# Attention scores by one 64-row matmul a head, even heads on the upper half of the TensorE array and odd heads on the lower

## The chip, the cores and the metric

The program runs on one core of one Trainium2 chip. The metric is the device time of one execution in microseconds (us), the median over several runs. The engines are named as the profile names them: PE is TensorE's matmul, PEld its load of the stationary operand, DVE is VectorE, ACT is ScalarE, POOL is GpSimd, SP is SyncE, which issues most DMAs.

## The reference

Eight batches of eight heads, 576 positions, 64 values a head. Keys and values are averaged over 8 neighbouring positions, so that 72 pooled positions are left; every query attends to them; the result goes through two feed-forward layers with 4608 tokens.

```python
k_p = k.reshape(B, H, Sp, 8, D).mean(axis=3)          # Sp = 72, D = 64
v_p = v.reshape(B, H, Sp, 8, D).mean(axis=3)
scores = scale * np.matmul(q, k_p.transpose(0, 1, 3, 2))
attn = softmax(scores)                                 # + 1e-9 in the sum
x = np.matmul(attn, v_p)  ->  (4608, 512)
h = relu(x @ w_in);  x = (h * h) @ w_out               # 512 -> 2048 -> 512
h = x @ w_in2;  g = where(h >= 1, h, where(h <= -1, 0, (h + 1)**2 / 4))
out = g @ w_out2
```

All is float32. The large products are made of three float32r products of a high and a low part each; the scores are plain float32 products.

## The kernel before

The 4608 tokens go through the attention and the first layer in nine chunks of 512 (`c`), each chunk in tiles of at most 128 tokens. A tile (`tokens`) goes through these steps: `t0` transposes its queries on PE (`qps`) and ACT copies them into `T.qT`, which holds for each pair `p` of heads the 128 rows "64 of the even head, 64 of the odd head"; then the scores, then the softmax (`soft`: DVE takes the maximum, then subtracts it, and `t3` has ACT take the exponent; for seven tiles `T.scalar` is set and ACT does one head at a time), then `t4` (DVE sums, inverts, multiplies into `A`), then `t56` (PE transposes `A` into `aps` and `lps`). `pv_two` and `pv_pair` multiply with the values (`pvps`), which gives the first layer's input x.

The scores use a block-diagonal matrix `kBD`: for each pair `p` of heads it is 128 rows by 144 columns, with the pooled keys of the even head in rows 0 to 63 and columns 0 to 71, those of the odd head in rows 64 to 127 and columns 72 to 143, and zeros, set once at the start by a DVE memset, in the two other blocks. One matmul with all 128 rows of contraction gives the scores of both heads of a pair. `k_T` (first batch) and `k_T_all` (the other seven) transpose the pooled keys on PE (`kps`), and ACT copies each half to its place:

```python
nc.scalar.activation(out=kBD[0:64, :, 0:SP_], in_=pv[0:64], func=AF.Copy, scale=ESCALE)
nc.scalar.activation(out=kBD[64:P, :, SP_:], in_=pv[64:P], func=AF.Copy, scale=ESCALE)
```

A tile's scores come in one of two forms. `t1` (the tiles of chunk 0 and the first three of chunk 1) takes one PSUM bank for two pairs of heads, does their two matmuls and then their softmax, and is called twice a tile. `t12` (the last two tiles of chunk 1 and all later ones) takes two banks, does all four matmuls at once and then the softmax of each bank. A tile that reaches over the end of a batch does its scores in two pieces, the first of which uses only the first 64 columns of `T.qT` as stationary operand. In all there are 40 pieces: 33 through `t12`, of which 29 have 128 tokens in the stationary operand and 4 have 64, and 7 through `t1`. `T.qT` is the stationary operand of each score matmul, the keys are the moving one.

The first layer runs beside this: for each of 16 slices `f` of its width there are 12 matmuls of 512 columns into `hp` (`h_mm`, lines 703 to 705) and, two slices later, 12 into four banks `y` (`y1_mm`, line 729). The order of the work on each engine is not written by hand: each piece of work is a generator that yields the engine it wants and a cost, and the class `Order` plays them through and issues them in the order that these costs give. The costs are numbers in the source (`yield "PE", 0.5` ahead of the scores of `t12`, `yield "ACT", 0.41` ahead of a copy of keys); changing one can move other instructions. After chunk 8 the second layer follows (`product`, line 963, and `y2_unit`, lines 972 to 974), which has no attention beside it.

Of the kernel before, what the change touches and what calls it, by code (L numbers as in the profile page):

```python
# [8 lines left out]
F32 = mybir.dt.float32  # L9
# [4 lines left out]
AF = mybir.ActivationFunctionType  # L14
ALU = mybir.AluOpType
AX = mybir.AxisListType
# [3 lines left out]
P = 128  # L20
# [131 lines left out]
def pooled_attention_moe_moe2(  # L152
# [13 lines left out]
    nc = tc.nc  # L166
    B, H, S, D = q.shape
# [3 lines left out]
    SP_ = S // POOL  # L171
    NP = H // 2
# [15 lines left out]
    ESCALE = 1.0 / (POOL * D ** 0.5)  # L188
# [15 lines left out]
    att = att_pool.__enter__()  # L204
# [5 lines left out]
    for d in range(3):  # L210
        m = mask[RL * d:RL * d + RL]
        nc.gpsimd.affine_select(
            out=m, in_=m, compare_op=ALU.is_ge, fill=0.0, base=0, channel_multiplier=1, pattern=[[-KL, HL]]
        )
        nc.gpsimd.affine_select(
            out=m, in_=m, compare_op=ALU.is_ge, fill=0.0, base=KL - 1, channel_multiplier=-1, pattern=[[KL, HL]]
# [10 lines left out]
    for c in range(NC):  # L227
        gs, col = [], 0
        while col < N:
            n = min(NG, N - col) if c > 1 else min(NG, N - col, S - (c * N + col) % S)  # L230
            ts = []
            for at in range(0, n, P):
                pieces, o, most = [], 0, min(P, n - at)
                while o < most:
                    b, start = divmod(c * N + col + at + o, S)
# [15 lines left out]
    def w_tile(f, dtype, name):  # L251
        return wpool.tile([P, 4 * DM], dtype, tag=f"w{f}", name=name)
# [77 lines left out]
        )  # L330


    kBD = att.tile([P, NP, 2 * SP_], F32, name="kBD")
    VH = att.tile([P, NP, 2, D], F32R, name="VH")
    VL = att.tile([P, NP, 2, D], F32R, name="VL")
    for t in (VH, VL):
        nc.vector.memset(t.bitcast(F32), 0.0)
    nc.vector.memset(kBD, 0.0)
    LV = att.tile([P, 2, HL, D], F32R, name="LV")[:3 * RL]
    att.tile([P, 8], F32, name="gap")  # L340

# [57 lines left out]
    def k_T(b, p):  # L399
        tag, ps = yield from take_ps("kps")  # L400
        kp = kp_t.pop((b, p))
        yield "PE", 0.35 * order.pe
        nc.tensor.transpose(ps[:, :SP_], kp[:SP_].rearrange("s h d -> s (h d)"), ident[:SP_, :SP_])
        yield "ACT", 0.45
        nc.scalar.activation(out=kBD[0:64, p, 0:SP_], in_=ps[0:64, :SP_], func=AF.Copy, scale=ESCALE)
        nc.scalar.activation(out=kBD[64:P, p, SP_:], in_=ps[64:P, :SP_], func=AF.Copy, scale=ESCALE)
        order.give("ps", tag)
        order.signal("k", b, p)

    def k_T_all(b):  # L410
        tag, ps = yield from take_ps("kps")
        yield "PE", 0.3
        for p in range(NP):
            kp = kp_t.pop((b, p))
            nc.tensor.transpose(
                ps[:, p * SP_:(p + 1) * SP_], kp[:SP_].rearrange("s h d -> s (h d)"), ident[:SP_, :SP_]
            )
        pv = ps[:, :NP * SP_].rearrange("q (p s) -> q p s", p=NP)
        yield "ACT", 0.41
        nc.scalar.activation(out=kBD[0:64, :, 0:SP_], in_=pv[0:64], func=AF.Copy, scale=ESCALE)  # L420
        yield "ACT", 0.41
        nc.scalar.activation(out=kBD[64:P, :, SP_:], in_=pv[64:P], func=AF.Copy, scale=ESCALE)
        order.give("ps", tag)
        for p in range(NP):
            order.signal("k", b, p)
# [44 lines left out]
    def take_ps(name):  # L470
        tag = yield "take", ("ps",)
        return tag, (psy if tag[0] == "y" else psa).tile([P, 512], F32, tag=tag, name=name)

    def tile_of(T, what):
# [12 lines left out]
        ps=("a0", "a1", "y0", "y1", "y2", "y3"), att=("",), at=("",), kv=("",), two=("",), yo=("", ""), job=("",) * 4  # L487
# [31 lines left out]
    def scores_of(T):  # L519
        if T.E is None:  # L520
            T.E = tile_of(T, "E")
            T.mx = att.tile([P, H, 1], F32, tag="mx", name="mx", bufs=4)
            if T.scalar:
                T.sm = att.tile([P, H, 1], F32, tag="sm", name="sm", bufs=4)

    def soft(T, ps, g, r):
        E, mx = T.E, T.mx
        hs = slice(4 * g, 4 * g + 4)
        sv = ps[r, :4 * SP_].rearrange("p (h s) -> p h s", h=4)

        yield "DVE", 0.47
        nc.vector.tensor_reduce(out=mx[r, hs], in_=sv, axis=AX.X, op=ALU.max, negate=True)
        if T.scalar:
            for h in range(4 * g, 4 * g + 4):
                yield "ACT", 0.3
                nc.scalar.activation(
                    out=E[r, h], in_=sv[:, h % 4], func=AF.Exp, bias=mx[r, h], accum_out=T.sm[r, h]
                )
        else:
            yield "DVE", 0.47  # L540
            nc.vector.tensor_tensor(
                out=E[r, hs], in0=sv, in1=mx[r, hs].to_broadcast([r.stop - r.start, 4, SP_]), op=ALU.add
            )

    def t1(T, g, r):
        scores_of(T)
        tag, ps = yield from take_ps("sps")
        yield "PE", order.pe
        for j in range(2):
            p = 2 * g + j  # L550
            nc.tensor.matmul(
                out=ps[:r.stop, j * 2 * SP_:(j + 1) * 2 * SP_], lhsT=T.qT[:, p, :r.stop], rhs=kBD[:, p, :],
                start=True, stop=True,
            )
        yield from soft(T, ps, g, r)
        order.give("ps", tag)

    def t12(T, r):
        scores_of(T)
        taken = []  # L560
        for g in range(2):
            taken.append((yield from take_ps("sps")))
        yield "PE", 0.5
        for g, (_, ps) in enumerate(taken):
            for j in range(2):
                p = 2 * g + j
                nc.tensor.matmul(  # L567
                    out=ps[:r.stop, j * 2 * SP_:(j + 1) * 2 * SP_], lhsT=T.qT[:, p, :r.stop], rhs=kBD[:, p, :],
                    start=True, stop=True,
                )  # L570
        for g, (tag, ps) in enumerate(taken):
            yield from soft(T, ps, g, r)
            order.give("ps", tag)

    def t3(T):
# [402 lines left out]
    with tc.manual_schedule():  # L978

        lent = []  # L980
        for i in range(4):
            t = w_tile(KF - 4 + i, F32, "lent").rearrange("p (e a n) -> p e a n", e=2, a=2)
            lent += [t[:, 0], t[:, 1]]
        qw = w_tile(11, F32, "qraw").rearrange("p (r n) -> p r n", r=QR)
        T, T1 = tiles[0], tiles[1]
# [4 lines left out]
        t = w_tile(8, F32R, "lent")  # L990
# [87 lines left out]
        def keys0(b, p, eng):  # L1078
            yield ev("k raw", b, p)
            yield from k_pool(b, p, eng)  # L1080
            yield from k_T(b, p)
# [25 lines left out]
        def keys_T(b, last):  # L1107
            yield ev("scores", last, b - 1)
            for p in range(NP):
                yield ev("kp", b, p)  # L1110
            yield from k_T_all(b)
# [20 lines left out]
        def tokens(t):  # L1132
# [27 lines left out]
            for b, _, o, m in t.pieces:  # L1160
                for p in range(NP):
                    yield ev("k", b, p)
                r = slice(o, o + m)
                if t in pace or t in T1[3:]:
                    yield from t12(t, r)
                else:
                    for g in range(2):
                        yield from t1(t, g, r)
                order.signal("scores", t, b)
# [294 lines left out]
        for i in range(C2 * PAIRS):  # L1464
            c, j = divmod(i, PAIRS)
            for k in range(M7):
# [14 lines left out]
                if loads2 and k in (2, 5):  # L1481
                    _, load, n = loads2.pop(0)
# [44 lines left out]
```

## Time and profile before

| | us |
|---|---|
| median of 3 runs | 1716.55 (1716.06 to 1721.89) |
| the profiled execution, its own time | 1715.73 |
| its span, first to last instruction | 1714.0 |
| PE busy | 1685.9 |
| ACT busy | 862.0 |
| DVE busy | 929.1 |

The profiled execution's time is its span and 1.7 us around it, and 0.8 us under the median of the runs. Line numbers in rows of the trace are those of the kernel before. In a row of a matmul, `128*64 128x144` means 128 rows of contraction, 64 columns of the stationary operand, and a moving operand of 128 partitions by 144 columns. A float32 matmul stands as two records in the trace: 160 score matmuls are written and 320 are recorded.

### The profile page before, as it was taken

How to read it: one execution, taken by the hardware profiler on the slowest of the kernel's cores; microseconds unless marked ns; L12 is line 12 of the kernel's file. 1: busy time of each engine (PE TensorE's matmuls, PEld its weight loads, DVE VectorE, ACT ScalarE, POOL GpSimd, SP SyncE). 2: the span in 40 equal slices, each digit the busy share in tenths (PEclk: the TensorE clock that was granted, in tenths of full speed). 3: DMA queues.
4: the chain of work that ended last, by engine and by line, in shares of the span. 5: the costliest groups of instructions: out<-in, count | busy, mean ns of one | idle time of the engine just before them, and what ended most of it. 6: DMA issues, size and time to landing. Idle time of an engine off the chain costs nothing.

```text
span 1714.0 us, 22862 instructions
## 1 busy us (share of the span) xinstructions
PE 1685.9 (98%) x8366; PEld 1463.2 (85%) x8366; DVE 929.1 (54%) x1811; ACT 862.0 (50%) x1704; POOL 170.3 (10%) x185
## 2 busy tenths in 40 slices
PE   5999999999999999999999999999999999999999
PEld 4888888888888888888888899899999899999897
DVE  7896757666666565655422344544444444444544
ACT  5885545545455555455333444544444444444544
POOL 3322221023111132210000000000000000000000
PEclk6899999999999999999999999999999999999999
DMA  9844767677766666666468464614424325225312
GB/s 247 238 172 129 231 204 230 207 233 225 232 223 194 216 211 205 210 181 206 129 232 299 180 232 147 229 54 151 163 74 156 133 74 181 108 74 203 111 50 86
DMA packets 207616, 302.44 MB, mean 176 GB/s; under 512 B 65552, under 2 KB 155920, under 8 KB 192912
## 3 DMA queue, kind: packets, MB, share of 16 engines
q1 hardware_dynamic: 202896, 292.59, 52.6%
q10 hardware_dynamic: 4608, 8.39, 1.3%
q8 instruction: 66, 1.08, 0.2%
q14 instruction: 46, 0.38, 0.1%
HBM read 219.68 MB, written 81.26 MB: 176 GB/s over the span
## 4 chain that ended last, share of the span: by engine, by line
PE 95%; DMA 3%; SPq 1%; DVE 1%; POOL 1%; ACT 0%; issue 0%; POOLq 0%
PE y L729 22%; PE h L963 21%; PE y L973 8%; PE y L972 8%; PE y L974 8%; PE hp L703 7%; PE hp L705 7%; PE hp L704 7%; PE pvps L666 2%; PE sps L567 2%; PE qps L511 1%; PE aps L616 1%; DMA qraw<-in_q_dram 1%; DMA kv<-in_v_dram 1%; DMA lent<-in_v_dram 0%; DMA w<-in_moe_w_in_dram 0%
## 5 line engine op out<-in xcount | busy, mean ns | idle before, releaser
L729 PE MATMUL y<-gh,w 128*128 128x512 f32 (+1 forms) x1168 | 302.5, 392 | 0.0
L963 PE MATMUL h<-xc,s 128*128 128x384 f32 x1440 | 290.0, 336 | 0.0
L963 PEld LDWEIGHTS h<-xc,s 128*128 128x128 f32 x1440 | 257.2, 188 | 19.2 <-DVE yo L1410 0.4
L729 PEld LDWEIGHTS y<-gh,w 128*128 128x128 f32 x1168 | 212.5, 188 | 40.4 <-issue 0.4
L703 PE MATMUL hp<-x,w 128*128 128x512 f32 (+1 forms) x584 | 232.3, 398 | 0.0
L704 PE MATMUL hp<-x,w 128*128 128x512 f32 (+1 forms) x584 | 226.6, 388 | 0.3 <-DVE w L301 0.3
L705 PE MATMUL hp<-x,w 128*128 128x512 f32 (+1 forms) x584 | 226.9, 388 | 0.0
L973 PE MATMUL y<-x,g 128*128 128x512 f32 x576 | 226.1, 392 | 0.0
L972 PE MATMUL y<-x,g 128*128 128x512 f32 x576 | 225.3, 391 | 0.0
L974 PE MATMUL y<-x,g 128*128 128x512 f32 x576 | 224.9, 391 | 0.0
L710 ACT ACTIVATE hp<-hp 128x512 f32<-128x512 f32 (+1 forms) x146 | 84.2, 577 | 269.6 <-PE hp L705 267.6
L721 DVE TENSOR_TENSOR gl<-hp,gh 128x512 fp32r<-128x512 f32 (+1 forms) x146 | 99.3, 680 | 146.5 <-ACT hp L719 145.3
L729 PE MATMUL y<-gl,w 128*128 128x512 f32 (+1 forms) x584 | 159.6, 388 | 0.0
L1402 ACT ACTIVATE g<-u 128x384 fp32r<-128x384 f32 x192 | 100.9, 526 | 93.1 <-DVE u L1395 92.1
L705 PEld LDWEIGHTS hp<-x,w 128*128 128x128 f32 x584 | 110.4, 189 | 23.0
L704 PEld LDWEIGHTS hp<-x,w 128*128 128x128 f32 x584 | 110.8, 190 | 20.9 <-DVE w L301 0.7
L703 PEld LDWEIGHTS hp<-x,w 128*128 128x128 f32 x584 | 110.8, 190 | 20.9 <-issue 0.8
L729 PEld LDWEIGHTS y<-gl,w 128*128 128x128 f32 x584 | 108.8, 188 | 23.1
L974 PEld LDWEIGHTS y<-x,g 128*128 128x128 f32 x576 | 108.1, 188 | 23.2
L1393 ACT ACTIVATE u<-h 128x384 f32<-128x384 f32 x48 | 23.6, 492 | 204.0 <-PE h L963 204.0
L1403 DVE TENSOR_TENSOR g<-u,g 128x384 fp32r<-128x384 f32 x192 | 106.1, 552 | 33.5 <-ACT g L1402 29.1
L717 ACT ACTIVATE gh<-hp 128x512 fp32r<-128x512 f32 (+1 forms) x146 | 86.2, 591 | 71.7 <-PE y L729 69.9
(157 smaller groups left out, 2430.5 us busy)
## 6 DMA issues: line engine op xcount, KB each, us to landing
x<-wD SPq DMA_DIRECT2D x48, 1024.0 KB
w<-wS SPq DMA_DIRECT2D x46, 1024.0 KB
xD<-job SPq DMA_DIRECT2D x64, 448.0 KB
xc<-xD SPq DMA_DIRECT2D x30, 768.0 KB
sD<-job SPq DMA_DIRECT2D x32, 448.0 KB
s<-sD SPq DMA_DIRECT2D x14, 1024.0 KB
xl<-xD SPq DMA_DIRECT2D x12, 768.0 KB
out_dram<-yo SPq DMA_DIRECT2D x35, 256.0 KB
```

Of the source, the lines that this page charges most:

```text
L703: nc.tensor.matmul(out=hp, lhsT=hi[:, cs], rhs=xh[kk], start=(kk == 0), stop=False)
L704: nc.tensor.matmul(out=hp, lhsT=lo[:, cs], rhs=xh[kk], start=False, stop=False)
L705: nc.tensor.matmul(out=hp, lhsT=hi[:, cs], rhs=xl[kk], start=False, stop=(kk == KD - 1))
L717: nc.scalar.activation(out=gh, in_=hp, func=AF.Square)
L721: nc.vector.tensor_tensor(out=gl, in0=hp, in1=gh, op=ALU.subtract)
L729: nc.tensor.matmul(out=ys[d][:, cols], lhsT=w[:, d * P:(d + 1) * P], rhs=v, start=start, stop=stop)
L963: nc.tensor.matmul(out=bank, lhsT=w, rhs=v, start=(first and kt == 0 and n == 0), stop=(kt == 1 and n == 2), skip_group_check=not first,)
L972: nc.tensor.matmul(out=ys[t], lhsT=lhs[0], rhs=w[e][:, 0], start=first, stop=False)
L973: nc.tensor.matmul(out=ys[t], lhsT=lhs[0], rhs=w[e][:, 1], start=False, stop=False)
L974: nc.tensor.matmul(out=ys[t], lhsT=lhs[1], rhs=w[e][:, 0], start=False, stop=last)
L1402: nc.scalar.activation(out=gh, in_=u, func=AF.Copy)
L1403: nc.vector.tensor_tensor(out=gl, in0=u, in1=gh, op=ALU.subtract)
```

## The change

The block-diagonal `kBD` goes, with its memset. `kT` holds the transposed pooled keys of a pair as they come out of the transpose: the even head in partitions 0 to 63, the odd head in 64 to 127, 72 columns a pair, so that one ACT copy takes the place of two in `k_T` and in `k_T_all` (the costs told to `Order` there fall from 0.45 and twice 0.41 to 0.25 and once 0.41). A score matmul is now for one head `(p, e)`: 64 rows of contraction, partitions 64e to 64e + 63 of `T.qT` and `kT`, and 72 columns. The bank is now chosen by `e`, even or odd, and no longer by the pair. `t1` does the four even or the four odd heads; `t12` goes through the pairs and does even and odd in turn, in two banks. So eight matmuls of 72 columns stand for four of 144. `soft` reads and writes every second head, by strided views; its instructions are the same in number and size.

```diff
-    kBD = att.tile([P, NP, 2 * SP_], F32, name="kBD")
+    kT = att.tile([P, 2, NP, SP_], F32, name="kT")[:, 0]
...
-    nc.vector.memset(kBD, 0.0)
...
-        yield "ACT", 0.45
-        nc.scalar.activation(out=kBD[0:64, p, 0:SP_], in_=ps[0:64, :SP_], func=AF.Copy, scale=ESCALE)
-        nc.scalar.activation(out=kBD[64:P, p, SP_:], in_=ps[64:P, :SP_], func=AF.Copy, scale=ESCALE)
+        yield "ACT", 0.25
+        nc.scalar.activation(out=kT[:, p], in_=ps[:, :SP_], func=AF.Copy, scale=ESCALE)
...
-        nc.scalar.activation(out=kBD[0:64, :, 0:SP_], in_=pv[0:64], func=AF.Copy, scale=ESCALE)
-        yield "ACT", 0.41
-        nc.scalar.activation(out=kBD[64:P, :, SP_:], in_=pv[64:P], func=AF.Copy, scale=ESCALE)
+        nc.scalar.activation(
+            out=kT, in_=ps[:, :NP * SP_].rearrange("q (p s) -> q p s", p=NP), func=AF.Copy, scale=ESCALE
+        )
...
-    def soft(T, ps, g, r):
-        E, mx = T.E, T.mx
-        hs = slice(4 * g, 4 * g + 4)
-        sv = ps[r, :4 * SP_].rearrange("p (h s) -> p h s", h=4)
+    def soft(T, ps, e, r):
+        E, mx = (t[r].rearrange("p (h e) s -> p e h s", e=2)[:, e] for t in (T.E, T.mx))
+        sv = ps[r, :NP * SP_].rearrange("p (h s) -> p h s", h=NP)
...
+    def scores_mm(T, p, e, ps, r):
+        d = slice(D * e, D * e + D)
+        nc.tensor.matmul(
+            out=ps[:r.stop, p * SP_:(p + 1) * SP_], lhsT=T.qT[d, p, :r.stop], rhs=kT[d, p], start=True, stop=True
+        )
+
+    def t1(T, e, r):
         scores_of(T)
         tag, ps = yield from take_ps("sps")
         yield "PE", order.pe
-        for j in range(2):
-            p = 2 * g + j
-            nc.tensor.matmul(
-                out=ps[:r.stop, j * 2 * SP_:(j + 1) * 2 * SP_], lhsT=T.qT[:, p, :r.stop], rhs=kBD[:, p, :],
-                start=True, stop=True,
-            )
-        yield from soft(T, ps, g, r)
+        for p in range(NP):
+            scores_mm(T, p, e, ps, r)
+        yield from soft(T, ps, e, r)
...
     def t12(T, r):
...
-        for g, (_, ps) in enumerate(taken):
-            for j in range(2):
-                p = 2 * g + j
-                nc.tensor.matmul(
-                    out=ps[:r.stop, j * 2 * SP_:(j + 1) * 2 * SP_], lhsT=T.qT[:, p, :r.stop], rhs=kBD[:, p, :],
-                    start=True, stop=True,
-                )
+        for p in range(NP):
+            for e, (_, ps) in enumerate(taken):
+                scores_mm(T, p, e, ps, r)
```

The changed costs move some instructions. On PE, in the middle of the program, a tile's scores stand between the matmuls of the first layer; this is the last such place (chunk 8), before and then of the change. `hp`, `y` and the numbered `w` are the first layer's banks and weights; `x4` and `x8` count matmuls in a row as they are written.

```order
L705 MATMUL hp<-x,w_7656 128x512
L567 MATMUL sps<-kBD,qT 128x144 x4
L703 MATMUL hp<-x,w_7656 128x512
L704 MATMUL hp<-x,w_7656 128x512
L705 MATMUL hp<-x,w_7656 128x512
```

```order
L699 MATMUL hp<-x,w_7800 128x512
L543 MATMUL sps<-kT,qT 128x72 x8
L697 MATMUL hp<-x,w_7800 128x512
L698 MATMUL hp<-x,w_7800 128x512
L699 MATMUL hp<-x,w_7800 128x512
```

Here only the scores themselves are different. At the start, on PE, things move: these are the transposes `aps` and `lps` of the 64-token first tile of chunk 1, before and then of the change.

```order
L703 MATMUL hp<-x,w_308 128x256
L704 MATMUL hp<-x,w_308 128x256
L705 MATMUL hp<-x,w_308 128x256
L729 MATMUL y_621<-gh,w_308 128x256 x2
L729 MATMUL y_622<-gh,w_308 128x256 x2
L729 MATMUL y_623<-gh,w_308 128x256 x2
L616 MATMUL aps<-ident,lent 128x64 x4
L622 MATMUL lps<-ident,lent 96x64 x2
L729 MATMUL y_624<-gh,w_308 128x256 x2
```

```order
L660 MATMUL pvps<-lent,VH 128x256
L660 MATMUL pvps<-lent,LV 128x256
L610 MATMUL aps<-ident,lent 128x64 x4
L616 MATMUL lps<-ident,lent 96x64 x2
L697 MATMUL hp<-x,w_313 128x256
L698 MATMUL hp<-x,w_313 128x256
L699 MATMUL hp<-x,w_313 128x256
```

They stood behind twelve `hp` matmuls and six `y` matmuls of the first layer; now they stand right behind the `pvps` matmuls and ahead of those twelve.

## Rows read from the trace of the kernel before

**Rows 1.** Page: busy time and share of each engine; the chain that ended last.

```profile
PE 1685.9 (98%) x8366; PEld 1463.2 (85%) x8366; DVE 929.1 (54%) x1811; ACT 862.0 (50%) x1704; POOL 170.3 (10%) x185
...
PE 95%; DMA 3%; SPq 1%; DVE 1%; POOL 1%; ACT 0%; issue 0%; POOLq 0%
```

**Rows 2.** Stretches: us from and to, length, busy, PEclk granted clock (1.00 is full).

```profile
45.00:105.00 60.00, 56.56 (x318) 48.93 (x317) 56.15 (x89) 51.23 (x135) 21.30 (x18) 0.92 0.79 240
105.00:860.00 755.00, 754.69 (x3761) 634.54 (x3760) 471.25 (x932) 396.84 (x748) 133.36 (x140) 1.00 0.65 200
```

**Rows 3.** Waits of PE, first from 105 to 860, then 0 to 105: total, times, longest.

```profile
PE hp L704 <- DVE w L301: 0.3, 1, 0.3
...
PE qps L511 <- DMA qraw<-in_q_dram: 9.7, 2, 6.7
```

**Rows 4.** Groups by line and shape: the scores.

```profile
L567 PE MATMUL sps<-kBD,qT 128*128 128x144 f32 x232 | 33.2, 286 | 0.0
...
L567 PE MATMUL sps<-kBD,qT 128*64 128x144 f32 x32 | 4.8, 292 | 0.0
```

**Rows 5.** L551 alone (the scores of t1) from 79 to 105, columns as in rows 2.

```profile
79.00:105.00 26.00, 2.62 (x16) 2.43 (x16) 1.00 0.78 262
```

**Rows 6.** PE in order of time: start, us, what, xcount. A 128-token piece.

```profile
833.07 0.40 PE L705 MATMUL hp<-x,w 128*128 128x512 f32 x1
833.31 1.15 PE L567 MATMUL sps<-kBD,qT 128*128 128x144 f32 x8
834.20 0.49 PE L703 MATMUL hp<-x,w 128*128 128x512 f32 x1
834.52 0.39 PE L704 MATMUL hp<-x,w 128*128 128x512 f32 x1
```

**Rows 7.** PE in order of time: 64-column matmuls with the values.

```profile
72.38 0.28 PE L666 MATMUL pvps<-AL,VH 128*128 128x64 f32 x1
72.49 0.28 PE L666 MATMUL pvps<-LT,LV 96*128 96x64 f32 x1
72.60 0.48 PE L703 MATMUL hp<-x,w 128*128 128x512 f32 x1
```

**Rows 8.** PE in order of time, and by form: transposes of keys, 72 columns.

```profile
727.59 0.41 PE L415 MATMUL kps<-ident,kp 72*128 72x72 f32 x4
...
L415 PE MATMUL kps<-ident,kp 72*128 72x72 f32 x28 | 3.2, 230 | 0.5 <-POOL kp L389 0.5
```

**Rows 9.** PE in order of time: a score piece of 64 columns of stationary operand.

```profile
131.95 0.39 PE L705 MATMUL hp<-x,w 128*128 128x512 f32 x1
132.27 1.20 PE L567 MATMUL sps<-kBD,qT 128*64 128x144 f32 x8
133.39 0.50 PE L703 MATMUL hp<-x,w 128*128 128x512 f32 x1
133.73 0.40 PE L704 MATMUL hp<-x,w 128*128 128x512 f32 x1
```

**Rows 10.** PE in order of time: transposes with 64 rows of contraction.

```profile
145.53 0.39 PE L705 MATMUL hp<-x,w 128*128 128x512 f32 x1
145.85 0.46 PE L616 MATMUL aps<-ident,A 64*128 64x64 f32 x4
```

**Rows 11.** PE, then DVE, in order of time near 60 us.

```profile
58.14 0.41 PE L666 MATMUL pvps<-lent,LV 96*128 96x256 f32 x1
...
61.56 0.41 DVE L599 TENSOR_TENSOR lent<-lent,sm 64x96 f32<-64x96 f32 x2
```

**Rows 12.** Two stretches of the start, columns as in rows 2.

```profile
41.00:47.80 6.80, 5.84 (x25) 4.98 (x26) 5.38 (x11) 5.39 (x21) 0.00 (x0) 0.50 1.07 345
...
54.70:61.40 6.70, 6.44 (x29) 6.28 (x30) 6.54 (x13) 6.30 (x17) 2.79 (x3) 0.50 0.16 44
```

**Rows 13.** By tile: the keys' copies and memset; ns min, median, max.

```profile
L422 ACT ACTIVATE kBD<-kps x7: 406/408/408, 71.6 to 728.7; 64x288 f32<-64x288 f32 x7
...
L338 DVE MEMSET kBD<- x1: 538/538/538, 2.1 to 2.1; 128x576 f32 x1
```

More of the change, by code (lines that the diff above doesn't have):

```diff
@@ L417, in k_T_all @@
             )
-        pv = ps[:, :NP * SP_].rearrange("q (p s) -> q p s", p=NP)
         yield "ACT", 0.41
-        nc.scalar.activation(out=kBD[0:64, :, 0:SP_], in_=pv[0:64], func=AF.Copy, scale=ESCALE)
-        yield "ACT", 0.41
-        nc.scalar.activation(out=kBD[64:P, :, SP_:], in_=pv[64:P], func=AF.Copy, scale=ESCALE)
+        nc.scalar.activation(
+            out=kT, in_=ps[:, :NP * SP_].rearrange("q (p s) -> q p s", p=NP), func=AF.Copy, scale=ESCALE
+        )
         order.give("ps", tag)
@@ L524, in scores_of @@
                 T.sm = att.tile([P, H, 1], F32, tag="sm", name="sm", bufs=4)
-    def soft(T, ps, g, r):
-        E, mx = T.E, T.mx
-        hs = slice(4 * g, 4 * g + 4)
-        sv = ps[r, :4 * SP_].rearrange("p (h s) -> p h s", h=4)
+    def soft(T, ps, e, r):
+        E, mx = (t[r].rearrange("p (h e) s -> p e h s", e=2)[:, e] for t in (T.E, T.mx))
+        sv = ps[r, :NP * SP_].rearrange("p (h s) -> p h s", h=NP)
         yield "DVE", 0.47
-        nc.vector.tensor_reduce(out=mx[r, hs], in_=sv, axis=AX.X, op=ALU.max, negate=True)
+        nc.vector.tensor_reduce(out=mx, in_=sv, axis=AX.X, op=ALU.max, negate=True)
         if T.scalar:
-            for h in range(4 * g, 4 * g + 4):
+            for h in range(NP):
                 yield "ACT", 0.3
                 nc.scalar.activation(
-                    out=E[r, h], in_=sv[:, h % 4], func=AF.Exp, bias=mx[r, h], accum_out=T.sm[r, h]
+                    out=E[:, h], in_=sv[:, h], func=AF.Exp, bias=mx[:, h], accum_out=T.sm[r, 2 * h + e]
                 )
@@ L541, in soft @@
             nc.vector.tensor_tensor(
-                out=E[r, hs], in0=sv, in1=mx[r, hs].to_broadcast([r.stop - r.start, 4, SP_]), op=ALU.add
+                out=E, in0=sv, in1=mx.to_broadcast([r.stop - r.start, NP, SP_]), op=ALU.add
             )
-    def t1(T, g, r):
+    def scores_mm(T, p, e, ps, r):
[4 more added lines that the diff above has]
+    def t1(T, e, r):
         scores_of(T)
@@ L560, in t12 @@
         taken = []
-        for g in range(2):
+        for e in range(2):
             taken.append((yield from take_ps("sps")))
         yield "PE", 0.5
-        for g, (_, ps) in enumerate(taken):
-            for j in range(2):
-                p = 2 * g + j
-                nc.tensor.matmul(
-                    out=ps[:r.stop, j * 2 * SP_:(j + 1) * 2 * SP_], lhsT=T.qT[:, p, :r.stop], rhs=kBD[:, p, :],
-                    start=True, stop=True,
-                )
-        for g, (tag, ps) in enumerate(taken):
-            yield from soft(T, ps, g, r)
+        for p in range(NP):
+            for e, (_, ps) in enumerate(taken):
+                scores_mm(T, p, e, ps, r)
+        for e, (tag, ps) in enumerate(taken):
+            yield from soft(T, ps, e, r)
             order.give("ps", tag)
```

## Prediction

> **What bounds the kernel now.** I read the page first. PE is busy for 98% of the span and makes up 95% of the chain that ended last, so TensorE sets the time; the reader should ask next whether that holds where the scores run. The table of stretches [rows 2] says that it does: from 105 to 860 us PE is busy for 754.69 of 755.00 us at the full granted clock (1.00, the 2.4 GHz level), and its waits on other engines there come to one of 0.3 us [rows 1, 3]. Every microsecond of PE work that is added or taken away between 105 and 860 therefore moves the end by as much. All 33 score pieces of `t12` lie there. ACT and DVE have room, and what they save counts only where PE waits for it. Before 45 us it is otherwise: PE waits 9.7 us for queries alone [rows 3], and between 45 and 105 it is idle for 3.44 us [rows 2].
>
> **The price of a pass.** The trace must give three prices: streaming, loading the stationary operand, and going from one shape of matmul to another.
>
> Streaming: a 128-token piece is eight records, each with a load and a matmul pass, two to a float32 product. They take 1.15 us, and the last has a length of 0.286, so starts are (1.15 - 0.286)/7 = 0.123 us apart, and eight take 0.98 [rows 4, 6]. With 64 columns of stationary operand, which takes less to load, the pace is (1.20 - 0.292)/7 = 0.13 [rows 4, 9]: no faster, so the pace is set by the 144 streamed columns. Four float32 passes of 72 columns stand (0.41 - 0.23)/3 = 0.06 apart [rows 8]. A pass of the change, at 72 columns, would thus stream in 0.06.
>
> Loading: the matmuls with the values have other weights each, 128 columns of them, and with only 64 columns to stream they still start at 72.38, 72.49 and 72.60 [rows 7]: 0.11 us apart, where 512 columns take 0.23. That is the price of a load of 128 columns, and it is the same for 128 rows and for 96. The transposes of [rows 8] also have 128 stationary columns and are not held to it, but they are another kind of matmul. So a pass of the change costs 0.11 if loads come one after another, because its 0.06 of streaming no longer covers the load.
>
> Shape: [rows 6] and [rows 9] are the same work between the same matmuls, once with 128 and once with 64 stationary columns. From the last `hp` matmul ahead to the second behind it takes 834.52 - 833.07 = 1.45 us and 133.73 - 131.95 = 1.78. Going to the narrower shape and back costs 0.33. For 64 rows of contraction the trace has only transposes, and going to them costs alike: 0.32 from the `hp` matmul to the first of them [rows 10], as in [rows 9], against 0.24 in [rows 6]. I take 0.33 for a visit to 64 rows.
>
> **The change, part by part.**
>
> A 128-token piece in `t12`: 16 passes where there were 8. I take loads as one after another, 16 x 0.11 = 1.76, less 0.98, plus 0.33 for the shape: +1.11 us. The 29 such pieces (232 records in eights [rows 4]) give +32.2 us. If the loads cost up to the 0.123 that they hid under before, it is 0.21 more a piece, +6.0 in all.
>
> A 64-token piece: its loads are half as wide, its passes stream in 16 x 0.06 = 0.96, and it pays for the change of shape already. Four pieces, about 0.
>
> `t1`: a call is all even or all odd heads, so its passes stay on one half of the array. 8 x 0.11 - 4 x 0.123 + 0.33 = +0.72 us. Four calls lie after 79 us (16 records in fours [rows 5]), where PE hardly waits: +2.9. The other ten come earlier, among waits for queries: I take 0, and at most 8 x 0.72 = 5.8 (the last two are narrow).
>
> The keys: one ACT copy of about 0.4 us goes for each of seven batches, and a memset of 0.54 us at the start [rows 13]. No PE wait on them is in the trace after 105 us, so 0; ACT and DVE were not the bound, and the first keys have to land anyway.
>
> The softmax: same instructions. Its first half starts later, since the even bank is now finished one pass before the odd one and no longer half way; the transposes of `A` that follow stand some 7 us behind the scores on PE, so 0 is taken.
>
> The moved instructions: in the middle of the program `Order` moves whole pieces of PE work past each other on an engine that is never idle: 0. At the start the transposes of the 64-token tile now stand ahead of twelve `hp` matmuls. They need `A`, which DVE finished at 61.56 + 0.41 = 61.97, while the `pvps` matmuls ahead of them end at about 58.35 [rows 11]. If `A` comes no sooner, PE stands for 3.6 us with the first layer queued behind; ACT and DVE order their work differently there too, so `A` may come in time. Against that, at most the 3.44 us of idle time go. Two stretches of the start run at a granted clock of 0.50 (1.2 GHz) with PE busy for 5.84 and 6.44 us [rows 12]; one such stretch more or less is 3 us. I take 0, with 4 either way.
>
> Sum: 32.2 + 2.9 = +35.1 us on the profiled execution's 1715.7, so 1750.8; the median of the runs is 0.8 above that execution, so 1751.6 us.
>
> A rule of the Trainium skill speaks against the size of this, and for the change. The page TensorEngine Tiling (Array Packing), section Key Properties, has tiles of the array load and multiply independently, in parallel. By it two loads would go at once in `t12`, and the time would be that of the first rival below. No row here has a matmul on the lower half of the array, so the trace neither confirms nor denies it.
>
> **Rivals.**
>
> *Loads of the two halves overlap.* In `t12` even and odd heads alternate, two passes each. If the second pass of one half and the first of the other load together, 16 passes take 8 x 0.11 = 0.88: 0.88 - 0.98 + 0.33 = +0.23 a piece, +6.7 for 29; the four narrow pieces stream side by side, 0.48 for 0.98, -2.0; `t1` does not alternate, +2.9. Together +7.6: 1724 us. For it: that the two halves have rows and banks of their own. Against it: in every row seen each load follows the matmul before it in order.
>
> *Not slower: neither load nor stream counts twice.* If a load of 64 rows needs no more than its streaming and the halves run side by side, also in `t12`, a piece is 16 x 0.06/2 = 0.48 - 0.98 + 0.33 = -0.17, 29 of them -4.9; with -2.0 for the narrow pieces and 4 x (0.48 - 0.49 + 0.33) = +1.3 for `t1`, -5.6: 1711 us. It decides once a piece's passes take under 0.98 - 0.33 = 0.65 us, or 0.04 a pass. Against it: the load of 96 rows cost what 128 do [rows 7].
>
> *Each change of half costs a change of shape.* A `t12` piece changes half seven times inside; at 0.33 each that is 2.3 us a piece, +67 over 29 and +9 over the four, on top of the forecast: about 1828 us. Against it: nothing in the rows; both halves have the same shape.
>
> *Something in between*: loads that overlap in part, 1730 to 1745.
>
> **How the numbers follow.** The forecast has 0.55, overlapping loads 0.27, not slower 0.06, the costly change of half 0.05, in between 0.07. The forecast's own range is 1745 to 1762: the start's 4 us below; above, the 6 of slower loads and the start's 4. The range given, 1719 to 1762, reaches down over most of the overlapping case; it leaves out the not-slower case, the costly halves and the lower tail of the overlapping one, some 0.18. A half per cent, 8.6 us, is about what a measurement of this kernel tells from no change. Over it: the forecast, in between, the costly halves, and four in ten of the overlapping case, which with its start lies on either side of that bound: 0.78. Faster by over 8.6: half of the not-slower case, with a good start, 0.03. The rest, 0.19, is within.
>
> **What would show it.** In the changed trace the 16 score matmuls of a 128-token piece should start 0.11 us apart, with loads one after another, and the stretch from the `hp` matmul ahead to the second behind should be near 2.56 us, where it was 1.45; the part of the program from the first `t12` piece to the start of line 963's counterpart should be some 32 us longer, and the second layer unchanged. PE should stay without waits there. The prediction is wrong if starts come in close pairs (the first rival), if they come at 0.06 or less, or if the first 100 us move by more than 4.

## The result and the profile after

The changed kernel takes 1731.96 us (median of four runs, 1731.03 to 1733.35). The kernel before, run beside it, takes 1718.92 us (1716.06 to 1721.89). That is 13.0 us more: a ratio of 1.0088 with an interval of 1.0073 to 1.0103. The runs of the kernel before come in two groups, near 1716 and near 1722 us (14 of all 55 in the upper one), so that a median of few of them can move by some us with the share of each. The time lies in the range that was given and on the side that was forecast, but the kernel lost 13 us where the sum said 35. The profiled execution took 1731.34 us, its span is 1729.6.

The page of the changed kernel: busy time of each engine, and the chain that ended last, by engine.

```profile
PE 1707.0 (99%) x8686; PEld 1471.7 (85%) x8686; DVE 930.6 (54%) x1810; ACT 860.8 (50%) x1693; POOL 165.9 (10%) x185
...
PE 92%; DMA 4%; SPq 1%; DVE 1%; POOL 1%; issue 0%; ACT 0%; ACTq 0%; POOLq 0%; DVEq 0%
```

PE still sets the time, with 320 more records than in [rows 1] (a pass is one record); ACT has lost 11 instructions, and no wait of PE in the kernel before was on a copy of keys.

The changed kernel's stretches, columns as in [rows 2]:

```profile
45.00:105.00 60.00, 56.37 (x300) 49.07 (x300) 52.68 (x82) 48.07 (x127) 21.59 (x18) 0.80 0.76 230
105.00:870.00 765.00, 763.55 (x4036) 632.36 (x4035) 474.69 (x934) 398.08 (x745) 127.93 (x140) 1.00 0.64 196
...
51.20:75.00 23.80, 21.95 (x101) 20.23 (x102) 21.64 (x34) 16.24 (x40) 10.26 (x10) 0.50 0.69 199
```

Two things differ from [rows 2]. From 105 us on PE is again at its full clock and hardly idle: 1.45 us in 765. So the score pieces there can be read from PE's own rows. But between 45 and 105 us the mean granted clock has fallen from 0.92 to 0.80, and one stretch of 23.8 us ran wholly at 0.50, the 1.2 GHz level. (0.92 - 0.80) x 60 = 7.2 us of full clock that the start had before and now has not.

The first 45 us, before and then of the change:

```profile
0.00:45.00 45.00, 24.62 (x103) 20.50 (x104) 31.96 (x65) 24.88 (x63) 15.63 (x27) 0.69 0.95 254
0.00:45.00 45.00, 31.38 (x141) 26.30 (x141) 31.77 (x65) 23.82 (x59) 16.39 (x27) 0.66 0.95 255
```

Up to 105 us PE is now idle for 13.62 + 3.63 = 17.3 us, where it was idle for 20.38 + 3.44 = 23.8. Longer waits are therefore not what the start lost in these two executions; PE is busy for longer, at a lower clock.

Nearly all of the 1.45 us from 105 us on are two waits of PE, by what ended them: total, times, longest.

```profile
PE sps L543 <- ACT qT L511: 0.8, 1, 0.8
PE pvps L660 <- ACT kT L417: 0.6, 1, 0.6
```

Now the scores themselves. PE of the changed kernel in order of time (start, us, what, xcount): a piece with a 64-token tile, then one with 128 tokens.

```profile
135.52 0.39 PE L699 MATMUL hp<-x,w 128*128 128x512 f32 x1
135.84 0.72 PE L543 MATMUL sps<-kT,qT 64*64 64x72 f32 x16
136.48 1.45 PE L723 MATMUL y<-gh,w 128*128 128x512 f32 x5
...
372.74 0.39 PE L699 MATMUL hp<-x,w 128*128 128x512 f32 x1
373.05 1.12 PE L543 MATMUL sps<-kT,qT 64*128 64x72 f32 x16
374.10 0.50 PE L697 MATMUL hp<-x,w 128*128 128x512 f32 x1
374.44 0.39 PE L698 MATMUL hp<-x,w 128*128 128x512 f32 x1
```

The 128-token piece, from the `hp` matmul ahead to the second behind, takes 374.44 - 372.74 = 1.70 us, where [rows 6] has 1.45: **+0.25 us**, and not +1.11. The narrow one, from the `hp` matmul ahead to the first matmul behind, takes 136.48 - 135.52 = 0.96, where [rows 9] has 133.39 - 131.95 = 1.44: **-0.48 us**.

The changed kernel's score matmuls in four windows of 0.11 us from the start of that 128-token piece: length, PE busy (passes in flight), PEld busy (loads in flight), clock.

```profile
373.04:373.15 0.11, 0.10 (x2) 0.10 (x2) 1.00 0.64 74
373.15:373.26 0.11, 0.11 (x4) 0.11 (x4) 1.00 0.00 0
373.26:373.37 0.11, 0.11 (x6) 0.11 (x4) 1.00 0.00 0
373.37:373.48 0.11, 0.11 (x8) 0.11 (x4) 1.00 0.00 0
```

Each window adds two passes, not one. In the single records of the trace they start in pairs, at 0 and 7 ns, 167 and 174, 279 and 285, 390 and 397, and their loads do too: an even head and an odd head at once, and the next pair 0.11 us later. 0.11 is still the price of a load of 128 columns, but the two halves pay it together. That is slightly more overlap than the first rival had, which paired the second pass of one half with the first of the other: here the very first two passes start together, and each half then keeps its own pace.

Last, PE of the kernel before in order of time, around a call of `t1` and at the start of the second layer:

```profile
78.94 0.40 PE L705 MATMUL hp<-x,w 128*128 128x512 f32 x1
79.17 0.66 PE L551 MATMUL sps<-kBD,qT 128*128 128x144 f32 x4
79.57 0.48 PE L703 MATMUL hp<-x,w 128*128 128x512 f32 x1
...
955.29 2.01 PE L963 MATMUL h<-xc,s 128*128 128x384 f32 x9
```

and the same place of the changed kernel, where line 957 answers to line 963:

```profile
970.93 1.66 PE L957 MATMUL h<-xc,s 128*128 128x384 f32 x7
```

All of the 15.6 us between the two spans have come by then: 970.93 - 955.29 = 15.6.

### The profile page after: what moved, and what is told of

The parts are those of the page before. It is cut to its first block, busy times and chain, and to the rows that moved or that the text cites. A ratio compares the mean times of both kernels' runs of the same rounds, so it can differ in the third digit from the quotient of the medians.

```text
span 1729.6 us, 23486 instructions
## 1 busy us (share of the span) xinstructions
PE 1707.0 (99%) x8686; PEld 1471.7 (85%) x8686; DVE 930.6 (54%) x1810; ACT 860.8 (50%) x1693; POOL 165.9 (10%) x185
## 4 chain that ended last, share of the span: by engine, by line
PE 92%; DMA 4%; SPq 1%; DVE 1%; POOL 1%; issue 0%; ACT 0%; ACTq 0%; POOLq 0%; DVEq 0%
PE y L723 21%; PE h L957 20%; PE y L967 8%; PE y L966 8%; PE y L968 8%; PE hp L697 7%; PE hp L699 7%; PE hp L698 7%; PE pvps L660 2%; PE sps L543 2%; DMA kv<-in_k_dram 1%; PE aps L610 1%; PE qps L508 1%; DMA kv<-in_v_dram 1%; DMA w<-in_moe_w_out_dram 1%; DMA x2T<-yo 1%
```

## The experiments

Two theories were tested. The first, the parallel one: the halves load and stream side by side, what is left of the scores' cost is a change of shape, and the rest of the 13 us is the new order of instructions at the start. Its rivals: that the passes go one after another and something else was saved; and that the order costs nothing, or costs it all. The second theory, on the low clock of the start, is told with the last three runs. "Before" in this section is the kernel before, run on the same chip beside each group: 1716.2 us (17 runs) for the first four experiments; 1717.18 (17) for one cost back, the quarters in the old order and the wider of the two fills; 1716.67 (17) for the quarters in the new order, the narrower fill and the changed kernel beside it.

### The new scores in the old order

The change altered two numbers of ACT's planned cost along with the key copies, 0.45 to 0.25, and one step of 0.41 fell away. `Order` places instructions by them. This kernel is the changed one with the old numbers, and its instructions on PE stand in the order of the kernel before.

```diff
-        yield "ACT", 0.25
+        yield "ACT", 0.45
         nc.scalar.activation(out=kT[:, p], in_=ps[:, :SP_], func=AF.Copy, scale=ESCALE)
 ...
             out=kT, in_=ps[:, :NP * SP_].rearrange("q (p s) -> q p s", p=NP), func=AF.Copy, scale=ESCALE
         )
+        yield "ACT", 0.41
```

> The 64-row scores with the costs of the kernel before told to the scheduler, so that every instruction stands in the order of the kernel before. Theory: the slower start of the changed kernel (its first 100 us end some 9 us later, in a stretch of 24 us at a granted clock of 0.50) comes of the moved instructions; then this kernel starts as the one before, and keeps only the price of the score pieces, some 5 to 7 us: 1724 to 1726 us against 1718.9. Rival: the 64-row passes themselves keep the granted clock down at the start; then the start is as long as in the changed kernel and the time near 1732.

Measured: 1724.56 us (six runs), ratio 1.0046 (1.0032 to 1.006): **+8.4 us for the new scores alone**. PE in order of time around a `t1` call and at the second layer's start, and then the stretch of the start:

```profile
77.84 0.39 PE L700 MATMUL hp<-x,w 128*128 128x512 f32 x1
78.16 1.11 PE L544 MATMUL sps<-kT,qT 64*128 64x72 f32 x8
79.20 0.50 PE L698 MATMUL hp<-x,w 128*128 128x512 f32 x1
...
963.43 2.53 PE L958 MATMUL h<-xc,s 128*128 128x384 f32 x12
```

```profile
45.00:105.00 60.00, 54.31 (x319) 45.94 (x318) 54.28 (x87) 48.52 (x130) 21.77 (x18) 0.97 0.75 226
```

The second layer starts 8.1 us late here. The `t1` call takes 79.20 - 77.84 = 1.36 us from `hp` to `hp`, against 79.57 - 78.94 = 0.63 before: +0.73, and four times that is 2.9. Within one half, then, passes do go one after another, 0.11 us apart in the single records. The sum of the three kinds of piece is 29 x 0.25 - 4 x 0.48 + 4 x 0.73 = 7.25 - 1.9 + 2.9 = +8.2 us, near the 8.4 that was measured. The clock at the start is 0.97: in this execution the scores alone have not brought the low clock of the changed kernel.

### The old scores in the new order

The reverse: the kernel before, with the changed kernel's numbers.

```diff
-        yield "ACT", 0.45
+        yield "ACT", 0.25
         nc.scalar.activation(out=kBD[0:64, p, 0:SP_], in_=ps[0:64, :SP_], func=AF.Copy, scale=ESCALE)
 ...
         nc.scalar.activation(out=kBD[0:64, :, 0:SP_], in_=pv[0:64], func=AF.Copy, scale=ESCALE)
-        yield "ACT", 0.41
```

> The scores of the kernel before (block-diagonal keys, 128 rows), with the costs of the changed kernel told to the scheduler, so that every instruction stands in the order of the changed kernel. Theory of the moved instructions: the first 100 us end some 9 us later than before, and the time is near 1728. Rival, the 64-row passes themselves: no change, near 1719.

Measured: 1720.36 us (twelve runs, 1716.32 to 1724.45), ratio 1.0021 (1.0011 to 1.0031): **+4.2 us for the order alone**. 8.4 + 4.2 = 12.6, against the 13.0 of the whole change. Its start, in the stretch and in PE's order of time:

```profile
45.00:105.00 60.00, 55.95 (x310) 48.16 (x310) 58.70 (x89) 52.04 (x134) 23.24 (x18) 0.91 0.74 232
```

```profile
957.10 2.53 PE L962 MATMUL h<-xc,s 128*128 128x384 f32 x12
```

This profiled execution is one of the better ones: it has lost only 1.8 us at the second layer, and its clock in the stretch is that of [rows 2]. So the median shows a price of the order, but the rows don't show where it was paid.

### The halves one after the other

The changed kernel with the two loops of `t12` exchanged: all even heads, then all odd ones. The work is the same, and no neighbours in the program lie on different halves, but for one pair.

```diff
-        for p in range(NP):
-            for e, (_, ps) in enumerate(taken):
+        for e, (_, ps) in enumerate(taken):
+            for p in range(NP):
                 scores_mm(T, p, e, ps, r)
```

> The changed kernel, with the scores of t12 for all four even heads first and then for all four odd heads, so that two passes in a row stay on one half of the array. Theory: the close pairs of starts (7 ns and 105 ns in turn) in the changed kernel are loads of the two halves that overlap, and they need the alternation; without it 16 passes take 16 x 0.11 = 1.76 us instead of some 0.85 to 0.9, which is +0.9 on 29 pieces: some 25 us over the changed kernel, 1757. Rival: what makes the pairs is the pair of passes of one float32 product, not the halves; then nothing changes, 1732.

Measured: 1745.72 us (four runs), ratio 1.0166 (1.0147 to 1.0184), so 13.8 us over the changed kernel by the two medians, and 16.5 if each is taken beside its own before. PE in order of time:

```profile
865.48 0.39 PE L699 MATMUL hp<-x,w 128*128 128x512 f32 x1
865.80 1.62 PE L543 MATMUL sps<-kT,qT 64*128 64x72 f32 x16
867.34 0.50 PE L697 MATMUL hp<-x,w 128*128 128x512 f32 x1
867.68 0.39 PE L698 MATMUL hp<-x,w 128*128 128x512 f32 x1
```

867.68 - 865.48 = 2.20 us, 0.50 over the 1.70 of the changed kernel, and 29 x 0.50 = 14.5 lies between the two differences. Alternating is therefore what made the passes cheap. Strictly serial passes would have added 0.88 a piece (8 x 0.11), and the single records show why it is less: the even half's passes start 0.11 us apart, and the odd half's first starts with the fifth of them, at 507 ns against 501. The last three even passes then run beside odd ones. (A record doesn't name its half; the pass at 507 ns is taken for the odd half's first because it is 327 ns long, like the first of the piece, while every other one is 272.)

### The change of shape alone

The kernel before, whose score matmuls in `t12` read only the upper 64 rows; the scores of the odd heads are left out by it. Eight passes of 144 columns remain, now with 64 rows.

```diff
-                    out=ps[:r.stop, j * 2 * SP_:(j + 1) * 2 * SP_], lhsT=T.qT[:, p, :r.stop], rhs=kBD[:, p, :],
+                    out=ps[:r.stop, j * 2 * SP_:(j + 1) * 2 * SP_], lhsT=T.qT[:D, p, :r.stop], rhs=kBD[:D, p, :],
```

> The kernel before, with the score matmuls of t12 cut to the upper 64 rows (the odd heads' scores are left out there and stay zero); number, columns and pace of the passes stay, only the shape is new. Theory: going to 64 rows and back costs 0.33 us a piece, as for 64 stationary columns, on 29 pieces: +9.6, 1728.5. Rival: a change of rows costs nothing beyond the pass, 1719.

Measured: 1729.09 us (four runs), ratio 1.0068 (1.0052 to 1.0083): +12.9. PE in order of time:

```profile
844.07 0.39 PE L705 MATMUL hp<-x,w 128*128 128x512 f32 x1
844.39 1.25 PE L567 MATMUL sps<-kBD,qT 64*128 64x144 f32 x8
845.56 0.50 PE L703 MATMUL hp<-x,w 128*128 128x512 f32 x1
845.90 0.40 PE L704 MATMUL hp<-x,w 128*128 128x512 f32 x1
```

845.90 - 844.07 = 1.83 us against the 1.45 of [rows 6]: a visit to 64 rows costs 0.38, near the 0.33 that was read from another shape. In the single records the passes keep their pace of 0.12 us from the second on, so this is the price of the change and not of slower passes. 29 x 0.38 = 11.0 of the 12.9; the other 1.9 were not followed up.

### One cost back

The changed kernel with only the first of the two numbers set back. PE's first 156 instructions then stand as in the kernel before, and later ones stand as in neither kernel.

```diff
-        yield "ACT", 0.25
+        yield "ACT", 0.45
         nc.scalar.activation(out=kT[:, p], in_=ps[:, :SP_], func=AF.Copy, scale=ESCALE)
```

> The changed kernel with one number of the scheduler set back: the cost told for the copy of the first batch's keys, 0.45 instead of 0.25. The first 156 rows of PE's order are then those of the kernel before; behind them the order is new in other places. Theory: the slower start comes of the rows that this number moves, and goes: near 1724 to 1726 us, like the new scores in the old order. Rival: it comes of what is moved later, or of the 64-row passes: near 1732.

Measured: 1739.93 us (four runs), ratio 1.0124 (1.0103 to 1.0144), which no theory had: some 8 to 10 us slower than the changed kernel. Two stretches, and PE's waits from 110 to 870 us (total, times, longest):

```profile
45.00:105.00 60.00, 54.97 (x327) 47.07 (x326) 55.39 (x85) 49.44 (x128) 17.61 (x15) 0.94 0.75 218
...
140.00:200.00 60.00, 50.46 (x250) 40.79 (x251) 27.73 (x53) 25.49 (x60) 19.34 (x21) 0.91 0.44 130
```

```profile
PE qps L508 <- DVE x L686: 6.1, 1, 6.1
PE lps L616 <- ACT AH L621: 1.7, 1, 1.7
PE hp L698 <- DVE w L301: 1.7, 3, 1.1
```

The start is mended (0.94), as expected. But between 140 and 200 us PE now stands idle for 9.5 us, most of it in the first two of these waits, which neither kernel has, and loses clock besides. So a planner's number moves the program in more places than the one it is named after, and the total of this run says nothing on the start.

### Quarters in the old order

If tiles of the array work side by side, four are better than two. This is the kernel of the first experiment, with each score matmul cut to 64 stationary columns: 64 by 64 tiles, 32 passes a piece.

```diff
-        nc.tensor.matmul(
-            out=ps[:r.stop, p * SP_:(p + 1) * SP_], lhsT=T.qT[d, p, :r.stop], rhs=kT[d, p], start=True, stop=True
-        )
+        for c in range(r.start, r.stop, 64):
+            nc.tensor.matmul(
+                out=ps[c:c + 64, p * SP_:(p + 1) * SP_], lhsT=T.qT[d, p, c:c + 64], rhs=kT[d, p], start=True, stop=True
+            )
```

> The new scores in the old order, and each matmul cut in two by stationary columns as well: 64 rows by 64 columns, tokens 0 to 63 and 64 to 127 apart, so that four quarters of the array share a piece. Theory: the quarters load and stream independently, as the halves do; a pass of 64 stationary columns loads in about 0.06 and streams in 0.06, so a piece's 32 passes take 8 x 0.06 = 0.5 where the halves took 0.85 to 0.9, and the 29 pieces give back about 0.38 each, some 11 us of the 1724.6 of the halves in the old order: 1712 to 1715, under the kernel before (1716.2). Rival: only the halves by rows are independent; then 16 x 0.06 = 0.96 a piece, 2 to 3 us more than the halves: 1727.

Measured: 1713.02 us (twelve runs), ratio 0.9972 (0.9959 to 0.9986): 4.2 us under the kernel before, and **faster than both kernels**, though than the kernel before by less than half a per cent. PE in order of time, a `t1` call and a 128-token piece:

```profile
79.25 0.39 PE L701 MATMUL hp<-x,w 128*128 128x512 f32 x1
79.57 0.72 PE L545 MATMUL sps<-kT,qT 64*64 64x72 f32 x16
80.22 0.50 PE L699 MATMUL hp<-x,w 128*128 128x512 f32 x1
...
830.24 0.39 PE L701 MATMUL hp<-x,w 128*128 128x512 f32 x1
830.56 0.73 PE L545 MATMUL sps<-kT,qT 64*64 64x72 f32 x32
831.22 0.50 PE L699 MATMUL hp<-x,w 128*128 128x512 f32 x1
831.56 0.40 PE L700 MATMUL hp<-x,w 128*128 128x512 f32 x1
```

The piece has four times the passes of the kernel before, and takes 831.56 - 830.24 = 1.32 us, 0.13 less. The `t1` call takes 80.22 - 79.25 = 0.97, 0.34 more than before. 29 x -0.13 - 1.9 + 4 x 0.34 = -3.8 - 1.9 + 1.4 = -4.3 us: near the measured 4.2, whose interval reaches from 2.4 to 7.0, out of PE's rows alone.

### Quarters in the new order

The same cut in the changed kernel itself, with its own costs; the diff is the one above.

> The quarters (64 rows by 64 stationary columns) with the costs of the changed kernel, so in its order. Against the quarters in the old order (1713.0 us) this gives the price of the order alone with 64-row passes in the tiles of the start. Theory, the order costs by itself what it cost with the old scores, 3 to 5 us: 1716 to 1718. Rival, it costs more together with 64-row passes, some 8 to 10: 1721 to 1723.

Measured: 1715.54 us (twelve runs), ratio 0.9989 (0.9977 to 1.0001), no difference that can be told. Beside its own before it is 1.1 us faster, the kernel with the old order 4.2: the order costs some 3 us here too, with intervals that overlap. The second pair agrees with the first, and alone it would not show a price.

### Filling the pauses at the start

The theory on the low clock of the start: that it falls because PE pauses there for the softmax, and that filling the pauses would hold it up. Two kernels put four matmuls of `ident` ahead of the transposes of chosen tiles, into the same bank, where the transposes write over them. The changed kernel itself ran beside the second.

```diff
+    def fill(T, ps):
+        for _ in range(4 if T in FILL else 0):
+            nc.tensor.matmul(out=ps[:, :P], lhsT=ident, rhs=ident, start=True, stop=True)
...
+        FILL = T[2:] + T1[:2]
```

> The changed kernel with extra work: ahead of the transposes of queries and of A of four early tiles, four matmuls of 128 columns by a constant, whose result is overwritten; 64 passes of 0.107 us at the full clock, 6.8 us in all, in part within waits of PE. Theory: at the start PE's pauses hold the granted clock at 0.50; with the pauses filled, the low stretch from 51 to 75 us shortens, and the kernel gets faster though it does more: 1722 to 1728. Rival: the clock follows something else; then what isn't hidden adds 3 to 7 us: 1735 to 1739.

The second, with `FILL = T[3:] + T1[:1]` and only ahead of `aps`:

> The changed kernel with extra work at two places only: ahead of the transposes of A of the last tile of chunk 0 (where PE waits 1.0 us for DVE) and of the first tile of chunk 1; 16 passes of 0.107 us, 1.7 us at the full clock, part of it inside the wait. Theory: the pauses of PE between 48 and 56 us bring on the low clock from 51 to 75 us, and filling them shortens it: 1724 to 1729. Rival: two fills are not enough, or the clock follows something else: 1732 to 1734.

> The changed kernel as it is, on the same chip as the two others of this call, so that each stands against it directly. No theory expects another time than its 1732.

Measured: 1729.72 us (six runs, ratio 1.0066, 1.0048 to 1.0085), 1729.85 (six, 1.0069, 1.0052 to 1.0086), and for the changed kernel 1729.83 (six, 1.0072, 1.0055 to 1.0089). The stretch from 45 to 105 us in each, first the wide fill:

```profile
45.00:105.00 60.00, 54.96 (x333) 48.97 (x334) 52.96 (x82) 47.27 (x125) 22.12 (x18) 0.89 0.75 228
```

then the fill at two places:

```profile
45.00:105.00 60.00, 56.85 (x315) 50.44 (x314) 52.46 (x81) 45.95 (x122) 21.51 (x18) 0.81 0.72 223
```

and the changed kernel as it is:

```profile
45.00:105.00 60.00, 55.51 (x299) 48.85 (x299) 52.07 (x80) 45.58 (x122) 21.17 (x18) 0.82 0.71 218
```

The narrow fill did nothing to the clock of the stretch. The wide one brought it from 0.82 to 0.89, (0.89 - 0.82) x 60 = 4.2 us of full clock, but the time stayed where it was. Its own matmuls in the same stretch, columns as before without DVE, ACT and POOL:

```profile
45.00:105.00 60.00, 5.07 (x32) 4.82 (x32) 0.89 0.75 228
```

They keep PE busy for 5.07 us, about as much as the clock gave back. The mean clock of whole runs agrees: 0.990 over the six runs with the wide fill, as in the kernel before, and 0.986 over the six of the changed kernel, on another chip. So the half of the theory on the clock is supported by the wide fill and not by the narrow one, and the half on the time failed: filling pauses with work that PE has to do as well won nothing. The third run says that the changed kernel's loss holds beside another set of runs of the kernel before: 13.2 us, where it was 13.0.

## Why the prediction missed the size

**The step that failed** is "I take loads as one after another, 16 x 0.11 = 1.76", +1.11 us a piece and +32.2 us in all. Passes that alternate between the halves load and stream in pairs, eight starts of 0.11 us instead of sixteen. The piece costs +0.25, within 0.02 of what the first rival had worked out (+0.23), and 29 of them +7.25 us in place of 32.2. The choice was argued from rows in which every load followed the matmul before it; but all of those rows have loads into rows of the array that their neighbours use too, so they could not speak on the point. The Trainium skill's rule, which stood beside the sum (TensorEngine Tiling (Array Packing), Key Properties: tiles load and multiply in parallel), would have given 1724 us. The pairs of starts, the exchanged loops and the quarters agree with it, and the new scores alone measured 1724.56. A rule that bears on just this operation deserved more than 0.27 against rows that did not.

**The prices were right.** 0.11 us for a load of 128 columns holds within a half: `t1`, which doesn't alternate, cost +0.73 a call where +0.72 was worked out. 0.33 for a change of shape was measured as 0.38 for 64 rows and 144 columns. It is all that a piece loses: the passes take 0.88 where they took 0.98, and the shape adds 0.33. By the wider price, 0.88 - 0.98 + 0.38 = +0.28, where +0.25 was measured.

**The narrow pieces** were taken as 0 and gave 4 x 0.48 = 1.9 us back, the rival's 2.0: there streaming sets the pace, and the halves stream side by side.

**The moved instructions** were taken as 0, with 4 either way. The order alone cost 4.2 us with the old scores, 13.2 - 8.4 = 4.8 with the new ones, and 3 with quarters: near the bound or just past it, and a term that should not have been 0. The place looked at, the transposes of the 64-token tile moved ahead of twelve `hp` matmuls, is not where it went. PE did not wait there for `A`, since the transposes follow the `pvps` matmuls almost at once:

```profile
58.55 0.41 PE L660 MATMUL pvps<-lent,LV 96*128 96x256 f32 x1
59.00 0.66 PE L610 MATMUL aps<-ident,lent 64*128 64x64 f32 x4
```

In the changed kernel's profile the start shows as lower clock, some 7 us of it in that one execution, and 8.2 + 7.2 = 15.4 would account for its 15.6. The mean clock of whole runs points the same way: 0.986 over the six runs of the changed kernel beside the fills against 0.989 over the six of the new scores in the old order, and 0.003 of 1730 us is some 5 us. Among those six runs the time follows the clock: 1725.6 us at 0.990, 1732.3 and 1732.8 at 0.983. With quarters it does not: the clock is 0.988 in both orders. The prediction had named such a stretch of low clock, at 3 us for one more or less, and left it inside the 4.

**The keys and the softmax** at 0 stand: the waits of PE from 105 us on come to 1.4 us, and only 0.6 of it ended with a copy of keys.

**The range.** The forecast's own range starts at 1745 in the text, while 1751.6 less the start's 4 is 1747.6; nothing above hangs on it.

**What is not shown:** why the clock is granted at 0.50 for longer in the new order. The old order with the same scores had 0.97 in the stretch, the new order with the old scores 0.91, and both together 0.80 and 0.82. The wide fill raised it, the narrow one didn't, and what sets it stays open. Open, too, are the half of the order's 4.2 us that the profile of the second experiment doesn't show, and why the order costs with quarters although the clock is the same.

## What to carry to other kernels

Cutting a contraction in two doubles the passes and adds a change of shape for each visit (here 0.33 to 0.38 us between wide matmuls), so it pays only if the pieces run side by side: issue them alternating, and cut the stationary columns as well, so that four tiles share the array. Ask of every row that speaks against overlap whether it could have overlapped at all. And where a planner places instructions by cost numbers, change the numbers apart from the work and time each by itself: here the numbers for a few ACT copies moved the time by 3 to 5 us, half of what the changed work cost, and setting only one of them back cost another 8 to 10.

## What the runs showed of the hardware beyond that

Passes on different halves did not start in program order, as far as the single records tell the halves apart. With all even heads ahead of all odd ones, the first odd pass started at 507 ns, beside the fifth even one at 501, while three even passes that stand ahead of it in the program started at 613, 725 and 836. So two halves overlap in part even where the program doesn't alternate, and a piece lost 0.50 us by it, not the 0.88 of serial passes.

Four tiles of 64 by 64 started 7 ns apart, and the next four some 62 ns after them (176, 183, 189, 196, then 238 ns in the single records). At that pace, 8 groups of 62 ns, 32 passes take 0.50 us, where the eight full passes before took 0.98; nearly all that is left of the piece's cost over that is the change of shape.
